# A Fourier mixing layer followed by two MLP layers: each chunk's tokens normalised and turned two chunks ahead, split one chunk ahead, one DMA each way, loads three chunks ahead

## The chip, the cores and the metric

One core of one Trainium2 chip runs the whole program. The metric is device time in microseconds (us), here that of the one core, the median of the runs shown.

The engines are TensorE (PE in the rows; its weight loads are PEld), VectorE (DVE), ScalarE (ACT), GpSimd (POOL) and SyncE (SP). Every DMA of this kernel is issued by SP. Each engine takes its instructions in the order in which the program lists them: an instruction that waits holds up everything listed behind it on that engine.

## What is computed

Two batches of 3136 tokens with 256 features pass through three layers. Cut to what matters:

```python
# 1: a filter in the frequency domain, along the tokens
X = rfft(x, axis=1)
Yr, Yi = shrink(Xr @ w_r - Xi @ w_i + b_r), shrink(Xr @ w_i + Xi @ w_r + b_i)
x = irfft(Yr + 1j * Yi, n=3136, axis=1)
# 2: normalise each token, MLP with 1024 hidden units, residual
xn = (x - mean) / sqrt(var + 1e-6) * g_ln
x = x + relu(xn @ w_ch1) @ w_ch2
# 3: 2-D Fourier transform over tokens and features, real part added, then as 2 without g_ln
u = x + real(fft(fft(x, axis=1), axis=2))
un = (u - mean) / sqrt(var + 1e-6)
return u + relu(un @ w2_ch1) @ w2_ch2
```

## The kernel before, in words

**Tiling.** The 6272 tokens are 49 tiles of 128. An MLP works on chunks of up to four tiles: `mlp1` (layer 2) has the chunks numbered 0 to 12 here, `mlp2` (layer 3) those numbered 13 to 25; most have four tiles, some three or two. Products are made in split precision: a value is held as a high part and a low part, and TensorE multiplies the parts one by one (lines 222 to 224).

**One chunk on TensorE.** `l1` makes eight groups of six matmuls with 512 columns (L222 to L224, into `psa`, three buffers). ScalarE evacuates each group with the relu (L686), VectorE then makes the low part (L687). `l2` makes, for each tile, eight pairs of matmuls (L703, L704, into `psb`), which VectorE adds to the residual (L707, L708). `store` sends the tile out (L716). On TensorE the order is: first two tiles of `l2` of chunk k, three groups of `l1` of chunk k+1, the other tiles of `l2`, five groups of `l1`. So between the last `l1` matmul of a chunk and the first of the next lie two `l2` tiles.

**What a chunk needs first.** `load` fetches its tokens `y` (L594), into a ring of four buffers; the buffer of chunk c was that of chunk c−4 and comes free when the last residual of c−4 is added. In `mlp2` each pair of tiles is read from the columns of `dX` and its mirror image as separate pieces of 64 and 128 KB, and a front end adds the transform: `Front.load` fetches `r` (L751/753), `stage_b` multiplies (L767), `dmix` multiplies again (L792) and adds into `y` on VectorE (L799 to L804; L801 is the first tile of a pair, L804 the mirrored one). Then `stats` (L604, L605), `norm` (four small VectorE steps L613 to L616, two ScalarE passes per tile L624 and L625 into `q`), `flip` (two 32x32 block transposes on VectorE, L640; each half stored to a scratch array `dT`, L644, and loaded back transposed, L646), and `trans`, the split (high part on ScalarE through L204, with a scaling pass L660 in `mlp1`; low part on VectorE, L212, both into `u0r`). Chunk 0 is transposed by TensorE instead (L668).

**Beside the chunks.** Around chunks 8 to 10 and 14 to 16 the token transform of layer 3 runs in steps (`Stage98`): loads `r<-dX`, POOL L371 to L373, a ScalarE copy L204 `u0r<-w`, matmuls L222 to L224 into `psc`, stores `dA<-o`. Around chunks 0 to 3 the inverse transform of layer 1 for batch 1 still runs (matmuls L322, stores `dY` L328 to L330), from which chunks 6 and later are loaded.

**What sets the order.** `run_mlp` emits the work of chunk k with the preparation of chunk k+1 attached by small tables (`STAGE_B_AT`, `DMIX_AT`, `STATS1_AT`, `STATS2_AT`, `LATE1`, `LATE2`), and loads chunk k+2. A scheduler then simulates a timeline and lists each engine's instructions as its model finds them ready; so an instruction may stand far ahead of where it was emitted.

Of the kernel before, what the change touches and what calls it, by code (L numbers as in the profile page):

```python
# [62 lines left out]
NF = DFF // 128  # L63
# [101 lines left out]
def fourier_moe_kernel(ctx, tc, x, w_r, w_i, b_r, b_i, g_ln, w11, w12, w21, w22,  # L165
# [415 lines left out]
    class Chunk:  # L581
# [25 lines left out]
        def norm(self):  # L607
# [13 lines left out]
            for i in range(nt):  # L621
                o, v = self.yn[:, i, :], y[:, i, :]
                if self.by_act:
# [3 lines left out]
                if not self.flipped:  # L627
                    o, v = (o.rearrange("p (h c j) -> p h j c", h=2, j=4), v.rearrange("p (h j c) -> p h j c", h=2, j=4))
# [4 lines left out]
        def flip(self, h):  # L633

            x = self.nt * 32
            if h == 0:
                self.d = next(dT_ring)
                self.xt, self.z = qslot(F32), qslot(F32)
            z = self.z[:, h * 512:h * 512 + 4 * x]
# [3 lines left out]
            dh = self.d[h][0:512 * x].rearrange("(p f) -> p f", p=128)  # L643
            sp.dma_start(out=dh, in_=z)  # L644
            v = bass.AP(dh.tensor, dh.offset, [[x, 128], [128 * x, 4], [1, x]])
            sp.dma_start(out=self.xt[:, h * 512:h * 512 + 4 * x].rearrange("p (i x) -> p i x", i=4), in_=v)  # L646

        def trans(self, c):
# [5 lines left out]
            if self.flipped:  # L654
                v = "p (i q t) -> p i q t"
                ps = self.xt[:, c * 512:c * 512 + n].rearrange("p (q i t) -> p i q t", q=4, t=32)
# [17 lines left out]
        def l1(self, f):  # L674
# [11 lines left out]
            nc.scalar.activation(out=h[:, 0:n], in_=ps[:, 0:n], func=AF.Relu)  # L686
# [211 lines left out]
    mlp1[0].flipped = False  # L898
# [34 lines left out]
    def run_mlp(chunks, nxt, hooks):  # L933

        allc = chunks + nxt
        for k, ch in enumerate(chunks):
            n = allc[k + 1] if k + 1 < len(allc) else None
            at = {}

            def put(part, i, f, *a):  # L940
                at.setdefault((part, i), []).append(lambda: f(*a))

            if n is not None and n.front is not None:
                i = 0
                for p, pr in enumerate(n.front.pairs):
                    put("l1", STAGE_B_AT[p], n.front.stage_b, p)
                    put("l1", DMIX_AT[p], n.front.dmix, p, n.y, i)
                    w = 2 if pr[0][1] else 1
                    for t in range(w):
                        put("l1", STATS2_AT[p], n.stats, i + t)  # L950
                    i += w
                late = LATE2
            elif n is not None:
                def stats(t, ch=ch, n=n):
                    with ExitStack() as es:
                        if ch is mlp1[0]:
                            es.enter_context(tc.issue_after(ch.rest[STATS1_AT[t]]))
                        n.stats(t)

                for t in range(4):  # L960
                    put("l1", STATS1_AT[t], stats, t)
                late = LATE1
            if n is not None:
                for (part, i), f, a in zip(late, (n.norm, n.flip, n.flip, n.trans, n.trans), ((), (0,), (1,), (0,), (1,))):
                    put(part, min(i, ch.nt - 1) if part == "l2" else i, f, *a)
# [65 lines left out]
    run_mlp(mlp1, mlp2[0:2], hooks)  # L1031
# [41 lines left out]
```

## Time and profile before

| | us |
|---|---|
| runs of the kernel before | 876.9, 877.44, 882.62 |
| their median | 877.44 |
| the profiled execution: its own time | 876.97 |
| the profiled execution: span of its trace | 875.2 |
| TensorE busy in the span | 812.8 |
| VectorE busy | 535.9 |
| ScalarE busy | 360.1 |
| POOL busy | 120.2 |

A span is the time from the first to the last instruction in the trace. In timeline rows the first number is the start in us, the second the duration, `x2` means that two like instructions in a row are shown as one, and the bracket at the end tells how long the engine was idle just before and what ended that. A matmul row can overlap the next, since matmuls are pipelined: their rate is read from the distance of starts.

### The profile page before, as it was taken

The page shows a single profiled execution, that of the slowest core. Times are in us where ns is not written, and L with a number is a line of the kernel's source. Part 1 is how long each engine was busy: PE and PEld are TensorE (multiplying, and loading weights), DVE is VectorE, ACT ScalarE, POOL GpSimd, SP SyncE. Part 2 cuts the span into 40 slices and gives each one's busy share as a digit, 9 for nine tenths or more (in the row PEclk, how much of TensorE's full clock was granted, in tenths as well). Part 3 has the DMA queues.
Part 4 walks back from the last instruction along what each step waited for, and adds up shares of the span by engine and source line. Part 5 has one row for each costly group of instructions (what it writes and reads, how often), then busy time and mean ns, then how long its engine had stood idle before and what let it go on. Part 6 is the DMA issues. An engine that isn't in the chain of part 4 may idle for free.

```text
span 875.2 us, 12158 instructions
## 1 busy us (share of the span) xinstructions
PE 812.8 (93%) x4268; PEld 672.4 (77%) x4268; DVE 535.9 (61%) x1262; ACT 360.1 (41%) x793; POOL 120.2 (14%) x152
## 2 busy tenths in 40 slices
PE   9999999989899999999999999988998888787996
PEld 4888878756778889887787877866886777676885
DVE  6589984597474678867576426525565655444432
ACT  1332465379374322552324325444455344132221
POOL 1112312300000000344100045353000000000000
PEclk9999999999989999999998999999999989999999
DMA  8641103414852122645422243533444321221001
GB/s 245 209 132 62 50 1 123 173 37 156 265 187 97 49 73 85 193 142 174 156 83 90 74 109 105 168 125 104 146 126 128 114 92 34 88 73 48 25 25 35
DMA packets 81777, 96.23 MB, mean 110 GB/s; under 512 B 17442, under 2 KB 60714, under 8 KB 81520
## 3 DMA queue, kind: packets, MB, share of 16 engines
q1 hardware_dynamic: 81716, 95.45, 35.1%
q8 instruction: 34, 0.56, 0.3%
q14 instruction: 27, 0.22, 0.1%
HBM read 57.41 MB, written 38.01 MB: 109 GB/s over the span
## 4 chain that ended last, share of the span: by engine, by line
PE 51%; DMA 20%; DVE 13%; ACT 6%; SPq 4%; POOL 3%; issue 2%; ACTq 0%; POOLq 0%; DVEq 0%
PE psb L703 13%; PE psa L222 7%; PE psb L704 7%; PE psa L223 6%; PE psa L224 6%; DMA yb<-dX 6%; DMA r<-dX 4%; PE psb L482 4%; DMA dT<-q 3%; DMA q<-dT 2%; DMA dA<-o 2%; DVE h L687 2%; SPq L328 2%; PE psc L303 2%; PE psa L450 2%
## 5 line engine op out<-in xcount | busy, mean ns | idle before, releaser
L686 ACT ACTIVATE h<-psa 128x512 fp32r<-128x512 f32 (+2 forms) x208 | 115.2, 570 | 205.5 <-PE psa L224 144.6
L687 DVE SCALAR_TENSOR_TENSOR h<-psa,h 128x512 fp32r<-128x512 f32 (+2 forms) x208 | 133.4, 651 | 76.8 <-ACT h L686 75.4
L703 PE MATMUL psb<-r2b,h 128*128 128x512 f32 x392 | 145.6, 416 | 7.0 <-ACT h L686 7.0
L703 PE MATMUL psb<-r3a,h 128*128 128x512 f32 x392 | 136.8, 397 | 1.4 <-ACT h L686 1.1
L222 PE MATMUL psa<-u0r,r2b 128*128 128x512 f32 (+2 forms) x208 | 84.9, 408 | 27.6 <-DVE h L687 27.1
L704 PE MATMUL psb<-r2b,h 128*128 128x256 f32 x392 | 108.8, 290 | 0.0
L704 PE MATMUL psb<-r3a,h 128*128 128x256 f32 x392 | 106.0, 283 | 0.8 <-DVE h L687 0.8
L703 PEld LDWEIGHTS psb<-r2b,h 128*128 128x128 f32 x392 | 76.3, 199 | 24.5 <-ACT h L686 8.3
L482 PE MATMUL psb<-wm,h 128*128 128x256 f32 (+1 forms) x600 | 88.8, 298 | 0.8 <-DVE w L488 0.8
L703 PEld LDWEIGHTS psb<-r3a,h 128*128 128x128 f32 x392 | 71.8, 188 | 17.5 <-ACT h L686 1.4
L222 PE MATMUL psa<-u0r,r3a 128*128 128x512 f32 (+2 forms) x192 | 77.4, 403 | 7.2 <-DVE h L687 7.0
L482 PEld LDWEIGHTS psb<-wm,h 128*128 128x128 f32 (+1 forms) x600 | 76.1, 189 | 8.6 <-issue 8.0
L223 PE MATMUL psa<-u0r,r2b 128*128 128x512 f32 (+2 forms) x208 | 82.1, 394 | 0.0
L704 PEld LDWEIGHTS psb<-r2b,h 128*128 128x128 f32 x392 | 78.2, 200 | 3.8
L224 PE MATMUL psa<-u0r,r2b 128*128 128x512 f32 (+2 forms) x208 | 81.1, 392 | 0.0
L704 PEld LDWEIGHTS psb<-r3a,h 128*128 128x128 f32 x392 | 73.6, 189 | 6.1 <-DVE h L687 1.5
L223 PE MATMUL psa<-u0r,r3a 128*128 128x512 f32 (+2 forms) x192 | 74.3, 387 | 0.0
L224 PE MATMUL psa<-u0r,r3a 128*128 128x512 f32 (+2 forms) x192 | 74.0, 387 | 0.0
L707 DVE TENSOR_TENSOR o<-psb,yb 128x256 f32<-128x256 f32 x74 | 29.5, 415 | 67.4 <-PE psb L704 67.3
L222 PEld LDWEIGHTS psa<-u0r,r2b 128*128 128x128 f32 x208 | 41.1, 197 | 37.0 <-DVE h L687 29.1
L204 ACT ACTIVATE yg<-psc 98x512 f32<-98x512 f32 (+2 forms) x58 | 48.3, 856 | 40.2 <-PE psc L502 26.7
L222 PEld LDWEIGHTS psa<-u0r,r3a 128*128 128x128 f32 x192 | 37.4, 195 | 17.6 <-DVE h L687 10.9
(125 smaller groups left out, 1292.3 us busy)
## 6 DMA issues: line engine op xcount, KB each, us to landing
dT<-q SPq DMA_DIRECT2D x42, 256.0 KB
q<-dT SPq DMA_DIRECT2D x42, 256.0 KB
s<-in_moe_w_ch_dram SPq DMA_DIRECT2D x16, 512.0 KB
r<-dX SPq DMA_DIRECT2D x32, 196.0 KB
dA<-o SPq DMA_DIRECT2D x32, 196.0 KB
dY<-yg SPq DMA_DIRECT2D x12, 512.0 KB
r<-dA SPq DMA_DIRECT2D x48, 128.0 KB
dX<-o SPq DMA_DIRECT2D x11, 512.0 KB
```

The costliest lines, as they stand in the source:

```text
L204: nc.scalar.activation(out=o, in_=i, func=AF.Copy, scale=scale)
L222: nc.tensor.matmul(out=ps, lhsT=lh, rhs=rh, start=first, stop=False)
L223: nc.tensor.matmul(out=ps, lhsT=ll, rhs=rh, start=False, stop=False)
L224: ins = nc.tensor.matmul(out=ps, lhsT=lh, rhs=rl, start=False, stop=last)
L303: nc.tensor.matmul(out=ps, lhsT=cam, rhs=self.raw[g // 2][:, e * 512:(e + 1) * 512], start=True, stop=True)
L328: sp.dma_start(out=dY[self.b][16 * c:16 * c + 16, :], in_=v[c:96:6, :])
L482: nc.tensor.matmul(out=ps[0:m, u * D:(u + 1) * D], lhsT=xv[:, o:o + m], rhs=wm_hl[wv][:, e, c, :], start=k == 0, stop=k == 11)
L686: nc.scalar.activation(out=h[:, 0:n], in_=ps[:, 0:n], func=AF.Relu)
L687: ins = nc.vector.scalar_tensor_tensor(out=l[:, 0:n], in0=ps[:, 0:n], scalar=0.0, in1=h[:, 0:n], op0=ALU.max, op1=ALU.subtract)
L703: nc.tensor.matmul(out=ps, lhsT=h[:, ts_], rhs=w2[:, f, :], start=f == 0, stop=False)
L704: nc.tensor.matmul(out=ps[:, 0:D], lhsT=l[:, ts_], rhs=w2[:, f, 0:D], start=False, stop=f == NF - 1)
L707: nc.vector.tensor_tensor(out=o, in0=ps[:, 0:D], in1=self.y[:, i, :], op=ALU.add)
```

## The change

The preparation of a chunk is taken apart. Statistics, front end, `norm` and `flip` are emitted two chunks ahead, with new table entries; the split is emitted one chunk ahead, behind the last evacuation (L687 of group 7) of the chunk before it; the load is emitted three chunks ahead, at the end of a chunk. `flip` stores and loads both halves with one DMA each way (512 KB where there were two of 256 KB). Chunk 1 is transposed by TensorE like chunk 0: eight more 128x128 matmuls and no `flip`. Line numbers of the changed kernel are 1 to 5 higher at the places below (L640 stays, L687 is L692, L707 is L712, L801 and L804 are L806 and L809, L212 is L213).

```diff
-STAGE_B_AT = (0, 1)
-DMIX_AT = (2, 3)
+STAGE_B_AT = (1, 3)
+DMIX_AT = (3, 5)
 STATS1_AT = (0, 1, 2, 3)
-STATS2_AT = (3, 4)
-LATE1 = (("l1", 4), ("l1", 5), ("l1", 6), ("l2", 0), ("l2", 1))
-LATE2 = (("l1", 5), ("l1", 6), ("l1", 7), ("l2", 1), ("l2", 2))
+STATS2_AT = (4, 6)
+NORM_AT = (4, 7)
+FLIP_AT = (1, 2)
+TRANS_AT = (0, 0)
...
         def flip(self, h):
...
-            dh = self.d[h][0:512 * x].rearrange("(p f) -> p f", p=128)
-            sp.dma_start(out=dh, in_=z)
-            v = bass.AP(dh.tensor, dh.offset, [[x, 128], [128 * x, 4], [1, x]])
-            sp.dma_start(out=self.xt[:, h * 512:h * 512 + 4 * x].rearrange("p (i x) -> p i x", i=4), in_=v)
+            if h == 0:
+                return
+            d = next(dT_ring).rearrange("h f -> (h f)")[0:1024 * x]
+            sp.dma_start(out=d.rearrange("(h p f) -> p h f", h=2, p=128),
+                         in_=self.z[:, 0:8 * x].rearrange("p (h f) -> p h f", h=2))
+            self.xt = qslot(F32)
+            sp.dma_start(out=self.xt[:, 0:8 * x].rearrange("p (i x) -> p i x", i=8),
+                         in_=bass.AP(d.tensor, d.offset, [[x, 128], [128 * x, 8], [1, x]]))
...
-    mlp1[0].flipped = False
+    mlp1[0].flipped = mlp1[1].flipped = False
...
-            n = allc[k + 1] if k + 1 < len(allc) else None
+            n, m, far = (allc[k + d] if k + d < len(allc) else None for d in (1, 2, 3))
...
+            def split(c, ch=ch, n=n):
+                with tc.issue_after(ch.relu), tc.issue_after(ch.rest[NF - 1]):
+                    n.trans(c)
+
+            if n is not None and n.flipped:
+                for c in range(2):
+                    put("l2", TRANS_AT[c], split, c)
+            todo = [m]
+            if n is mlp1[1]:
+                todo = [n, m]
+            for n_ in todo:
...
+                put("l1", NORM_AT[two], n_.norm)
+                if n_.flipped:
+                    for h in range(2):
+                        put("l2", FLIP_AT[h], n_.flip, h)
+                else:
+                    for c in range(2):
+                        put("l2", ch.nt - 1, n_.trans, c)
...
-            if k + 2 < len(allc):
-                allc[k + 2].load()
             for i in range(ch.nt):
                 ch.l2(i)
                 ch.store(i)
...
+            if far is not None:
+                far.load()
...
-    run_mlp(mlp1, mlp2[0:2], hooks)
+    mlp1[2].load()
+    run_mlp(mlp1, mlp2[0:3], hooks)
```

**Place 1, VectorE, the front end of chunk 25.** Before, these rows stand in `l2` of chunk 21, whose tiles are the L707/L708 rows; L801, L804 and L604 belong to chunk 25, whose `y` takes over the buffer that those L707 read.

```order
L707 TENSOR_TENSOR o<-psb,yb 128x256 x2
L708 TENSOR_TENSOR o<-psb,o 128x256 x2
L801 TENSOR_TENSOR yb<-w,yb 128x256
L604 BN_STATS st<-yb 128x6
L605 BN_AGGR mv<-st 128x2
L707 TENSOR_TENSOR o<-psb,yb 128x256
L804 TENSOR_TENSOR yb<-w,yb 128x256
L708 TENSOR_TENSOR o<-psb,o 128x256
L604 BN_STATS st<-yb 128x6
L687 SCALAR_TENSOR_TENSOR h<-psa,h 128x512 x2
```

In the changed kernel the rows of chunk 25 stand in `l2` of chunk 22 (the L712/L713 rows) and behind the first evacuation of chunk 23 (the L692 at the top).

```order
L692 SCALAR_TENSOR_TENSOR h<-psa,h 128x512
L208 COPY w<-psc 128x2
L208 COPY w<-w 128x1
L804 TENSOR_TENSOR w<-w,psc 128x127
L805 TENSOR_TENSOR w<-w,psc 128x127
L806 TENSOR_TENSOR yb<-w,yb 128x256
L809 TENSOR_TENSOR yb<-w,yb 128x256
L605 BN_STATS st<-yb 128x6 x2
L712 TENSOR_TENSOR o<-psb,yb 128x256
```

The addition into the mirrored tile (L804, now L809) moved from the chunk whose buffer its `y` inherits to the chunk after that; the chunks before it, 20 to 24, read alike.

**Place 2, VectorE, the split of chunk 25.** Before, the split (L212) stands ahead of the last evacuation of chunk 23: these are that chunk's evacuations, and its first `l2` tiles behind them.

```order
L687 SCALAR_TENSOR_TENSOR h<-psa,h 128x512 x4
L212 TENSOR_TENSOR u0r<-q,u0r 128x256 x2
L687 SCALAR_TENSOR_TENSOR h<-psa,h 128x512
L707 TENSOR_TENSOR o<-psb,yb 128x256 x2
L708 TENSOR_TENSOR o<-psb,o 128x256 x2
```

In the changed kernel it stands behind the last evacuation of chunk 24.

```order
L692 SCALAR_TENSOR_TENSOR h<-psa,h 128x512 x5
L213 TENSOR_TENSOR u0r<-q,u0r 128x256 x2
L712 TENSOR_TENSOR o<-psb,yb 128x256 x2
L713 TENSOR_TENSOR o<-psb,o 128x256 x2
L692 SCALAR_TENSOR_TENSOR h<-psa,h 128x256
```

The split moved later by one chunk and one evacuation, to the last place ahead of the chunk that reads it (the 256-wide L692 is that chunk's first evacuation).

**Place 3, VectorE, the first statistics of batch 1's later chunks.** Before, the statistics of chunk 6 (the L604 rows, `yb` loaded from `dY`) stand in `l2` of chunk 1.

```order
L687 SCALAR_TENSOR_TENSOR h<-psa,h 128x512
L640 STREAM_TRANSPOSE q<-q 128x4x4x32 x2
L687 SCALAR_TENSOR_TENSOR h<-psa,h 128x512
L707 TENSOR_TENSOR o<-psb,stg 128x256 x2
L708 TENSOR_TENSOR o<-psb,o 128x256 x2
L604 BN_STATS st<-yb 128x6 x3
L605 BN_AGGR mv<-st 128x2 x2
L604 BN_STATS st<-yb 128x6 x2
```

In the changed kernel they stand at the beginning of `l2` of chunk 2.

```order
L692 SCALAR_TENSOR_TENSOR h<-psa,h 128x512 x5
L640 STREAM_TRANSPOSE q<-q 128x4x4x32 x2
L213 TENSOR_TENSOR u0r<-w,u0r 128x512 x2
L605 BN_STATS st<-yb 128x6 x3
L712 TENSOR_TENSOR o<-psb,u0r 128x256
L606 BN_AGGR mv<-st 128x2 x2
L712 TENSOR_TENSOR o<-psb,u0r 128x256
```

They moved by seven evacuations of chunk 2, about one run of `l1`; the stores of `dY` that the loads wait for moved too, since batch 1's last inverse steps now end ahead of the second tile of chunk 1's `l2` instead of during its `l1`.

On SP the loads of a `mlp2` chunk's `y` stay where they were, among the stores of chunk c−4; between them stand the one store to `dT` and, two or three rows later, the one load from it. Each engine has about as many instructions as before, ScalarE somewhat fewer.

## Rows read from the trace of the kernel before

**Rows 1.** The page: the span and the first engine's busy time, share, instructions.

```profile
span 875.2 us, 12158 instructions
...
PE 812.8 (93%) x4268; PEld 672.4 (77%) x4268; DVE 535.9 (61%) x1262; ACT 360.1 (41%) x793; POOL 120.2 (14%) x152
```

**Rows 2.** By stretch: length; busy of PE, PEld, DVE, ACT, POOL; granted clock; DMA.

```profile
256.00:356.00 100.00, 99.72 (x541) 86.90 (x540) 68.45 (x146) 34.64 (x72) 0.00 (x0) 1.00 0.25 81
...
715.00:806.00 91.00, 75.22 (x357) 62.38 (x356) 42.90 (x112) 28.55 (x66) 0.00 (x0) 0.92 0.23 70
```

**Rows 3.** What TensorE waited for: line, awaited; total us, times, longest us.

```profile
PE psa L222 <- DVE h L687: 34.3, 12, 5.0
```

**Rows 4.** Timeline of TensorE: five of the nine long waits.

```profile
242.44 0.79 PE L222 MATMUL psa<-u0r,r3a 128*128 128x512 f32 x1 [4.07 <-DVE h L687]
...
477.19 0.79 PE L222 MATMUL psa<-u0r,r3a 128*128 128x512 f32 x1 [2.07 <-DVE h L687]
...
671.20 0.79 PE L222 MATMUL psa<-u0r,r2b 128*128 128x512 f32 x1 [4.31 <-DVE h L687]
...
697.61 0.44 PE L222 MATMUL psa<-u0r,r2b 128*128 128x384 f32 x1 [3.46 <-DVE h L687]
...
793.80 0.73 PE L222 MATMUL psa<-u0r,r2b 128*128 128x512 f32 x1 [4.98 <-DVE h L687]
```

**Rows 5.** Timeline of VectorE around the last of them.

```profile
786.03 0.42 DVE L707 TENSOR_TENSOR o<-psb,yb 128x256 f32<-128x256 f32 x1 [1.24 <-PE psb L704]
792.06 0.42 DVE L804 TENSOR_TENSOR yb<-w,yb 128x256 f32<-128x256 f32 x1 [5.61 <-DMA yb<-dX]
```

**Rows 6.** Timeline of SP: the load that this L804 waited for.

```profile
783.88 0.55 SPq L594 DMA_DIRECT2D yb<-dX  x1
```

**Rows 7.** VectorE's idle time ahead of line 804: total us, times.

```profile
  DMA yb<-dX: 26.2, 6
```

**Rows 8.** Timeline of TensorE: two `l2` tiles, then matmuls behind the wait.

```profile
783.02 0.39 PE L703 MATMUL psb<-r2b,h 128*128 128x512 f32 x1
...
788.55 0.28 PE L704 MATMUL psb<-r2b,h 128*128 128x256 f32 x1
...
797.31 0.40 PE L224 MATMUL psa<-u0r,r2b 128*128 128x512 f32 x1
797.55 0.39 PE L222 MATMUL psa<-u0r,r2b 128*128 128x512 f32 x1
```

**Rows 9.** Timeline of VectorE at the first long wait.

```profile
238.54 1.08 DVE L604 BATCH_NORM_STATS2 st<-yb 128x6 f32<-128x256 f32 x3 [6.21 <-DMA yb<-dY]
```

**Rows 10.** Timeline of SP: a store to `dT` and its load, other loads between.

```profile
660.75 1.06 SPq L644 DMA_DIRECT2D dT<-q  x2
661.85 0.45 SPq L751 DMA_DIRECT2D r<-dA  x1
666.86 0.37 SPq L646 DMA_DIRECT2D q<-dT  x1
```

**Rows 11.** Timeline of ScalarE: three waits behind which relus stood.

```profile
473.87 0.63 ACT L204 ACTIVATE u0r<-q 128x512 fp32r<-128x512 f32 x1 [6.89 <-DMA q<-dT]
...
574.60 0.63 ACT L204 ACTIVATE u0r<-w 98x512 fp32r<-98x512 f32 x1 [7.33 <-POOL w L373]
...
669.42 0.52 ACT L204 ACTIVATE u0r<-q 128x384 fp32r<-128x384 f32 x1 [7.81 <-DMA q<-dT]
```

**Rows 12.** Timeline of TensorE: the two long waits on the relu.

```profile
575.77 0.80 PE L703 MATMUL psb<-r2b,h 128*128 128x512 f32 x1 [3.36 <-ACT h L686]
...
610.49 0.80 PE L703 MATMUL psb<-r2b,h 128*128 128x512 f32 x1 [3.62 <-ACT h L686]
```

**Rows 13.** Timeline of VectorE: the low part of a split.

```profile
475.84 0.69 DVE L212 TENSOR_TENSOR u0r<-q,u0r 128x512 fp32r<-128x512 f32 x1 [0.29 <-ACT u0r L204]
```

**Rows 14.** The page's groups: busy time, mean ns of one, idle before, releaser.

```profile
L686 ACT ACTIVATE h<-psa 128x512 fp32r<-128x512 f32 (+2 forms) x208 | 115.2, 570 | 205.5 <-PE psa L224 144.6
L687 DVE SCALAR_TENSOR_TENSOR h<-psa,h 128x512 fp32r<-128x512 f32 (+2 forms) x208 | 133.4, 651 | 76.8 <-ACT h L686 75.4
```

More of the change, by code (lines that the diff above doesn't have):

```diff
@@ L622, in norm @@
                 o, v = self.yn[:, i, :], y[:, i, :]
+                if not self.flipped:
+                    o, v = (o.rearrange("p (h c j) -> p h j c", h=2, j=4), v.rearrange("p (h j c) -> p h j c", h=2, j=4))
                 if self.by_act:
@@ L626, in norm @@
                     continue
-                if not self.flipped:
-                    o, v = (o.rearrange("p (h c j) -> p h j c", h=2, j=4), v.rearrange("p (h j c) -> p h j c", h=2, j=4))
                 eng = nc.gpsimd if i in APPLY_POOL and self is mlp1[0] else nc.vector
@@ L636, in flip @@
             if h == 0:
-                self.d = next(dT_ring)
-                self.xt, self.z = qslot(F32), qslot(F32)
-            z = self.z[:, h * 512:h * 512 + 4 * x]
+                self.z = qslot(F32)
+            z = self.z[:, h * 4 * x:(h + 1) * 4 * x]
             nc.vector.transpose(out=z.rearrange("p (j i t) -> p i j t", j=4, t=32),
@@ L655, in trans @@
                 v = "p (i q t) -> p i q t"
-                ps = self.xt[:, c * 512:c * 512 + n].rearrange("p (q i t) -> p i q t", q=4, t=32)
+                ps = self.xt[:, c * n:(c + 1) * n].rearrange("p (q i t) -> p i q t", q=4, t=32)
                 h, l = (a[:, c, 0:n].rearrange(v, q=4, t=32) for a in (self.xh, self.xl))
@@ L685, in l1 @@
             h, l = hl[:, 0:512], hl[:, 512:1024]
-            nc.scalar.activation(out=h[:, 0:n], in_=ps[:, 0:n], func=AF.Relu)
+            ins = nc.scalar.activation(out=h[:, 0:n], in_=ps[:, 0:n], func=AF.Relu)
+            self.relu = getattr(ins, "ins", ins)
             ins = nc.vector.scalar_tensor_tensor(out=l[:, 0:n], in0=ps[:, 0:n], scalar=0.0, in1=h[:, 0:n],
@@ L936, in run_mlp @@
         for k, ch in enumerate(chunks):
-            n = allc[k + 1] if k + 1 < len(allc) else None
+            n, m, far = (allc[k + d] if k + d < len(allc) else None for d in (1, 2, 3))
             at = {}
             def put(part, i, f, *a):
[L941 to L962, printed above, removed]
@@ L963, in run_mlp @@
-            if n is not None:
-                for (part, i), f, a in zip(late, (n.norm, n.flip, n.flip, n.trans, n.trans), ((), (0,), (1,), (0,), (1,))):
-                    put(part, min(i, ch.nt - 1) if part == "l2" else i, f, *a)
+                at.setdefault((part, min(i, ch.nt - 1) if part == "l2" else i), []).append(lambda: f(*a))
+            def split(c, ch=ch, n=n):
[4 more added lines that the diff above has]
+                    put("l2", TRANS_AT[c], split, c)
@@ new lines, in run_mlp, with stats @@
+            todo = [m]
+            if n is mlp1[1]:
+                todo = [n, m]
+            for n_ in todo:
+                if n_ is None:
+                    continue
+                two = n_.front is not None
+                if two:
+                    i = 0
+                    for p, pr in enumerate(n_.front.pairs):
+                        put("l1", STAGE_B_AT[p], n_.front.stage_b, p)
+                        put("l1", DMIX_AT[p], n_.front.dmix, p, n_.y, i)
+                        w = 2 if pr[0][1] else 1
+                        for t in range(w):
+                            put("l1", STATS2_AT[p], n_.stats, i + t)
+                        i += w
+                else:
+                    def stats(t, ch=ch, n_=n_):
+                        with ExitStack() as es:
+                            if ch is mlp1[0]:
+                                es.enter_context(tc.issue_after(ch.rest[STATS1_AT[t]]))
+                            n_.stats(t)
+                    for t in range(4):
+                        put("l1", STATS1_AT[t], stats, t)
+                put("l1", NORM_AT[two], n_.norm)
+                if n_.flipped:
+                    for h in range(2):
+                        put("l2", FLIP_AT[h], n_.flip, h)
+                else:
+                    for c in range(2):
+                        put("l2", ch.nt - 1, n_.trans, c)
```

## The prediction

> **What bounds the kernel now.** I read the page first. TensorE is busy for 812.8 of 875.2 us, 93%, and no other engine comes near [rows 1]. So TensorE is the bound, and what a change can win is the time in which it stands still or runs slowly. The table by stretches tells where that is. From 256 to 356 us TensorE is busy for 99.72 of 100 us at full clock: an undisturbed stretch of chunks wastes nothing. From 715 to 806 us it is busy for 75.22 of 91, at a mean clock of 0.92 [rows 2].
>
> Next the list of what TensorE waited for. One row holds most: the first matmul of an `l1` group waiting for VectorE's evacuation L687, 34.3 us in 12 waits [rows 3]. Nine are long, 33.2 us together (the other three make 1.1); five are shown, and the four left out lie in the late stretch between the last two shown [rows 4]. An evacuation is short work, so the question is what stood ahead of it on its engine. The timelines around the waits answer:
>
> - The six from 697.61 to 793.80. In the last one SP issues a load of `y` at 783.88 [rows 6]. VectorE ends a residual addition at 786.45, then is idle for 5.61 us until that load has landed, and only at 792.06 makes L804, the addition into the mirrored tile of chunk 25 [rows 5]. L708 and two L687 are queued behind it (place 1 of the order). Issue to use is 792.06 − 783.88 = 8.2 us. The view of that line confirms that it is one mechanism: six waits, 26.2 us of idle VectorE [rows 7].
> - 242.44: the same with `bn_stats`, which is listed ahead of the evacuations and waits 6.21 us for a load from `dY` [rows 9].
> - 477.19 and 671.20: ScalarE's first step of a split waits 6.89 and 7.81 us for the flipped tokens to come back [rows 11]; relus are queued behind it, so L687 is late as well. At 671.20 the store to `dT` was issued at 660.75 and SP could send the load only at 666.86 [rows 10].
>
> Each long wait has a second cost. Behind that of 793.80 the granted clock is at the lower level: nine matmuls start from 793.80 to 797.31, eight distances in 3.51 us, 0.44 each, against 0.24 from 797.31 to 797.55 [rows 4, 8]. That is 8 × 0.2 = 1.6 us. The mean clock of 0.92 over 91 us says that 2 × 0.08 × 91 = 14.6 us were spent at the lower level in a stretch with four long waits and the slow matmuls behind them, so 3.6 us for each [rows 2]. Matmuls that run at half speed lose half of that, 1.8. I take 1.8 us for each wait; the example's 1.6 is the lower bound, and 2 the upper, were all nine like the worst.
>
> **The change, part by part.**
>
> *Front end and statistics two chunks ahead, loads three ahead.* The buffer ring still has four places, so loads cannot come much earlier; SP keeps them among the stores of chunk c−4. What moves is the consumer: L804 of chunk 25 stood one residual addition behind the one that frees its buffer, and now stands a whole chunk later (place 1 of the order). The first and the last matmul of two `l2` tiles start at 783.02 and 788.55; with 0.1 for the last, two tiles take 5.6 us [rows 8]; a chunk of four tiles is twice that plus 48 `l1` matmuls at 0.24, 11.2 + 11.5 = 22.7 us. A load that needs 8.2 us has 22 to do it. Six waits go: 26.2 us of VectorE's idle time, 22.8 of TensorE's (the six are 33.2 less 4.07, 2.07, 4.31) [rows 4, 7].
>
> *Split behind the last evacuation.* A split that waits can no longer hold up evacuations of the chunk before. The flip of a chunk is emitted in `l2` two chunks ahead; up to the split lie about two `l2` tiles and one run of `l1`, 5.6 + 11 = 16.6 us. The slow case took from 660.75 to 669.42, 8.7 us [rows 10, 11]. So the waits of 477.19 and 671.20 go too, 6.4 us.
>
> Its new price: nothing but two `l2` tiles, 5.6 us, now lies between the last `l1` matmul and the first that needs the split. Behind that matmul come a relu (0.57), the last L687 (0.65), two ScalarE copies (0.63 each) and two L212 (0.69 each) [rows 11, 13, 14]. ScalarE needs 0.57 + 2 × 0.63 = 1.8, VectorE ends at 0.57 + 0.65 + 2 × 0.69 = 2.6, or 3.2 if a copy is late. In `mlp1` two scaling passes make it about 4. Slack: 2.4 us, and 1.5 in `mlp1`. I cost it at nothing. If the cover were gone, each chunk would stand still for the whole chain.
>
> *One DMA each way.* Fewer issues on SP (twenty-odd chunks × 2). Off the path while the flip has its 16 us: zero; bounds from one issue saved (1.06 for two, so 0.5 us [rows 10]) to the load coming later by half of the 6.1 us from the stores to the load's issue, 3 us of a slack of 8 [rows 10].
>
> *Chunk 1 on TensorE, chunk 2 beside it.* Eight small matmuls. By the nearest rows they lie between 0.24 of a 512-column matmul and 0.79 of a slow one [rows 4, 8]: 2 to 6 us if none overlaps; I take 2, since they replace nothing. The statistics of chunk 6 move back by one run of `l1`, about 11 us, but so do the inverse's last steps and with them the `dY` stores and the loads (place 3 of the order). The lead stays what it was, between a wait gone (0) and the 6.21 us of now [rows 9]; I put back 3, so that of 4.07 + 1.8 about 3 remains gained.
>
> *The token transform around chunks 14 to 16.* Its two waits, 3.36 and 3.62, come from ScalarE's copy waiting for POOL (7.33 at 574.60) [rows 11, 12]. The change moves other work around them, not their loads. I leave them; bounds: they and their slow matmuls go (7.0 + 3.6 = 10.6 us), or they grow by as much.
>
> **The sum.** Nine waits 33.2 and 9 × 1.8 = 16.2: −49.4. Added: +2 (transposes), +3 (chunk 6), +1 (places where more work stands ahead of an evacuation near chunk 8). Span 875.2 − 43.4 = 831.8. The profiled execution took 876.97, 1.8 more than its span, and is within 0.5 us of the median 877.44; so **833.6 us**. Its own range, with the terms' bounds: 820 to 850.
>
> One rule would put the gain elsewhere. The load of 783.88 brings 128 KB and is not used before 8.2 us later [rows 5, 6]. The Trainium skill ("DMA: Bandwidth & Descriptors", Anatomy of one DMA) fits 2.0 us plus bytes over 436 GB/s for a DMA, an estimate of 2.3 us here, measured on the other descriptor path. By it the load would be there before L804's turn, there would be no wait to remove and the sum would lose 22.8 + 10.8; the trace differs, and decides.
>
> **Rivals.**
>
> *The token transform's waits go as well, and the start costs nothing.* For it: the split no longer shares ScalarE's queue with the steps ahead of the last evacuation. Against: POOL and its loads stay. 833.6 − 10.6 − 5 = 818. Chance 0.15.
>
> *SP gives back a third to half.* A load from `dT` waits on SP for its store: 666.86 against 661.85 + 0.45, 4.6 us [rows 10]. In the changed order the next `y` loads stand behind it. With a lead of 22 us less 8.2 there is room for two such waits, so only loads that also meet the transform's would be late. Half of the 33.6 us for the six waits comes back: about 850; or the statistics of chunks 6 to 9 stall in a row, 6.21 each for two more, the same size. Chance 0.15. The same page of the Trainium skill says that a DMA's semaphore wait is done by the issuing sequencer ahead of dispatch; SP's 4.6 us agree.
>
> *The split becomes a stall in each chunk.* This is the other side. If from the last `l1` matmul to the end of the split it takes more than 5.6 us, TensorE stops once per chunk, 24 times. What could stretch it: front-end steps that stand ahead of the split on VectorE and wait for a `dmix` product, or flipped tokens that are not back. At 1.8 us late per chunk the 43 us are used up; at 2.2, or 7.8 us of chain, 24 × 2.2 = 53 and the kernel is slower by over 1%, 886. Against: 2.6 to 4 us by rows. Chance 0.07.
>
> *The load is what is late, wherever its consumer stands.* If loads are issued later in the new order than the buffer allows, behind stores that wait for residuals, the wait only moves: within 1%, about 874. The order of SP speaks against it. Chance 0.06.
>
> **How the numbers follow.** My forecast has 0.57, lying within 820 to 850. Faster by over 1% (below 868.7; about 1% is what can be told from no change here): 0.57 + 0.15 + 0.15 = 0.87. Same 0.06, slower 0.07. For 8 in 10 I take the forecast's own range and go down to 814 for the first rival and up to 857 for the second; outside are the last two, 0.13, and some of the edges.
>
> **What would show it.** In the profile after: no wait of L809 for `yb<-dX` above 1 us; TensorE's wait on VectorE's evacuation below 10 us instead of 34.3; the stretch before the last chunks as dense as 256 to 356, clock 1.00. A wait of ScalarE on POOL near chunks 14 to 16 still there. For the split: the first `l1` matmul of a chunk follows the second `l2` tile without a wait on ScalarE's or VectorE's `u0r`. If TensorE's waits list `u0r` with two dozen entries, the third rival is right; if L809 still waits, the fourth.

## The result, and the profile after

The changed kernel takes 819.25 us (median of four runs, 817.12 to 819.83) against 877.17 us of the kernel before, timed beside it: a ratio of 0.933, 95% interval 0.928 to 0.938. The forecast was 833.6 with a range of 814 to 857 and 0.87 for faster by over 1%. Direction and mechanism held; the gain is 58 us where 43 were forecast.

The page of the kernel after: span, busy time of the engines, and TensorE's granted clock in 40 slices (9 is 0.9 or more).

```profile
span 817.4 us, 12025 instructions
...
PE 791.3 (97%) x4276; PEld 658.9 (81%) x4276; DVE 538.9 (66%) x1260; ACT 364.1 (45%) x791; POOL 120.2 (15%) x152
...
PEclk9999999999999999999999999999989999999999
```

The work is nearly the same; TensorE's busy time fell by 21.5 us all the same [rows 1]. The granted clock accounts for that (see the last section): one slice in 40 is left below 0.9. By stretch, in the columns of [rows 2]:

```profile
530.00:590.00 60.00, 60.00 (x322) 50.85 (x320) 34.78 (x87) 31.94 (x69) 28.69 (x49) 1.00 0.48 141
590.00:625.00 35.00, 28.92 (x126) 23.18 (x124) 15.23 (x34) 12.66 (x28) 3.75 (x8) 0.85 0.41 118
...
720.00:810.00 90.00, 90.00 (x496) 77.92 (x495) 47.90 (x122) 31.09 (x72) 0.00 (x0) 1.00 0.21 56
```

The last 90 us answer to the stretch of 75.22 busy us in 91 [rows 2]: now 90.00 of 90 at clock 1.00. The stretch 530 to 590, the token transform of batch 1 among the chunks, is full as well. Nearly all that TensorE still loses in layer 3, by standing still or at the lower clock, lies between 590 and 625. What TensorE waited for, the longest two entries (line, awaited; total us, times, longest):

```profile
PE psc L772 <- DMA r<-dA: 4.8, 2, 4.3
PE psa L223 <- DVE h L692: 4.0, 4, 1.9
```

34.3 us of waits on VectorE's evacuation [rows 3] became 4.0, and a wait on a load of the front end is new. The view of L809 (L804 before) has no releaser under "sat idle", where 26.2 us in six waits stood [rows 7]:

```profile
L809 DVE TENSOR_TENSOR yb<-w,yb x24: 412/419/420, 445.4 to 755.1; 128x256 f32<-128x256 f32 x24
its engine sat idle before it (us, times) until:
who waited for it (us, times):
```

Now the end of a late chunk, which shows the split in its new place. ScalarE, VectorE and TensorE between chunks 23 and 24:

```profile
765.76 0.60 ACT L690 ACTIVATE h<-psa 128x512 fp32r<-128x512 f32 x1 [0.76 <-PE psa L225]
766.25 1.14 ACT L205 ACTIVATE u0r<-q 128x512 fp32r<-128x512 f32 x2
```

```profile
766.39 0.69 DVE L692 SCALAR_TENSOR_TENSOR h<-psa,h 128x512 fp32r<-128x512 f32 x1 [0.67 <-ACT h L690]
767.00 1.28 DVE L213 TENSOR_TENSOR u0r<-q,u0r 128x512 fp32r<-128x512 f32 x2
```

```profile
765.33 0.39 PE L225 MATMUL psa<-u0r,r2b 128*128 128x512 f32 x1
...
771.17 0.39 PE L223 MATMUL psa<-u0r,r2b 128*128 128x512 f32 x1
```

The last `l1` matmul of chunk 23 starts at 765.33; the split is done at 768.28; the first `l1` matmul of chunk 24 starts at 771.17. A chain of 2.9 us stands in a cover of 5.8, and 2.9 are to spare.

Where the gain lies in the program, by the start of the last `l2` matmul of a chunk in either trace (us):

| after chunk | before | changed | gain so far | gain in the part |
|---|---|---|---|---|
| 2 | 265.8 | 261.7 | 4.1 | 4.1 |
| 14 | 555.9 | 542.8 | 13.1 | 9.0 |
| 16 | 624.4 | 603.7 | 20.7 | 7.6 |
| 17 | 654.4 | 637.2 | 17.2 | −3.5 |
| 25 | 867.8 | 810.3 | 57.5 | 40.3 |

The parts do not cut the work quite alike. By the traces, 12, 15 and 12 `l1` matmuls of the next chunk stand ahead of the last `l2` tile of chunks 14, 16 and 17 in the changed kernel, and none in the kernel before; at 0.23 us each that is 2.8 to 3.5 us made one part earlier.

### The profile page after: what moved, and what is told of

The parts are those of the page before. It is cut to its first block, busy times and chain, and to the rows that moved or that the text cites. A ratio compares the mean times of both kernels' runs of the same rounds, so it can differ in the third digit from the quotient of the medians.

```text
span 817.4 us, 12025 instructions
## 1 busy us (share of the span) xinstructions
PE 791.3 (97%) x4276; PEld 658.9 (81%) x4276; DVE 538.9 (66%) x1260; ACT 364.1 (45%) x791; POOL 120.2 (15%) x152
## 4 chain that ended last, share of the span: by engine, by line
PE 76%; DMA 9%; DVE 8%; ACT 3%; SPq 2%; issue 1%; POOL 1%; ACTq 0%; POOLq 0%
PE psb L708 20%; PE psb L709 10%; PE psa L223 10%; PE psa L224 10%; PE psa L225 9%; PE psb L483 4%; PE psc L772 3%; PE psc L323 2%; PE psc L304 2%; PE psc L503 2%; PE psc L797 1%; DMA cb<-in_cb_dram 1%; PE psa L451 1%; DMA h<-in_x_dram 1%; DMA r<-dA 1%
## 5 line engine op out<-in xcount | busy, mean ns | idle before, releaser
L692 DVE SCALAR_TENSOR_TENSOR h<-psa,h 128x512 fp32r<-128x512 f32 (+2 forms) x208 | 134.4, 654 | 91.5 <-ACT h L690 89.9
L708 PE MATMUL psb<-r3a,h 128*128 128x512 f32 x392 | 137.5, 399 | 0.6 <-DVE o L713 0.6
L708 PE MATMUL psb<-r2b,h 128*128 128x512 f32 x392 | 137.7, 398 | 0.0
L709 PE MATMUL psb<-r2b,h 128*128 128x256 f32 x392 | 106.0, 281 | 0.0
L708 PEld LDWEIGHTS psb<-r3a,h 128*128 128x128 f32 x392 | 71.6, 188 | 16.8 <-issue 1.5
L708 PEld LDWEIGHTS psb<-r2b,h 128*128 128x128 f32 x392 | 71.9, 188 | 14.7
L223 PE MATMUL psa<-u0r,r2b 128*128 128x512 f32 (+2 forms) x208 | 81.9, 394 | 0.0
L224 PE MATMUL psa<-u0r,r2b 128*128 128x512 f32 (+2 forms) x208 | 80.0, 385 | 0.0
L225 PE MATMUL psa<-u0r,r2b 128*128 128x512 f32 (+2 forms) x208 | 79.6, 384 | 0.0
L709 PEld LDWEIGHTS psb<-r2b,h 128*128 128x128 f32 x392 | 73.9, 189 | 3.2
L712 DVE TENSOR_TENSOR o<-psb,yb 128x256 f32<-128x256 f32 x74 | 30.6, 422 | 69.2 <-PE psb L709 68.4
L223 PE MATMUL psa<-u0r,r3a 128*128 128x512 f32 (+2 forms) x176 | 67.1, 382 | 4.0 <-DVE h L692 4.0
L224 PE MATMUL psa<-u0r,r3a 128*128 128x512 f32 (+2 forms) x176 | 66.2, 376 | 0.0
L225 PE MATMUL psa<-u0r,r3a 128*128 128x512 f32 (+2 forms) x176 | 63.8, 380 | 0.0
L213 POOL TENSOR_TENSOR h<-w 128x512 f32<-128x512 f32 (+1 forms) x26 | 34.1, 1314 | 109.9 <-DVE w L490 76.4
```

The source lines that it names most:

```text
L213: ins = eng.tensor_tensor(out=o, in0=a, in1=b, op=ALU.subtract)
L223: nc.tensor.matmul(out=ps, lhsT=lh, rhs=rh, start=first, stop=False)
L224: nc.tensor.matmul(out=ps, lhsT=ll, rhs=rh, start=False, stop=False)
L225: ins = nc.tensor.matmul(out=ps, lhsT=lh, rhs=rl, start=False, stop=last)
L692: ins = nc.vector.scalar_tensor_tensor(out=l[:, 0:n], in0=ps[:, 0:n], scalar=0.0, in1=h[:, 0:n], op0=ALU.max, op1=ALU.subtract)
L708: nc.tensor.matmul(out=ps, lhsT=h[:, ts_], rhs=w2[:, f, :], start=f == 0, stop=False)
```

## The experiments

Each run was timed in turns with the kernel before on one chip; the chips differ by half a per cent or so, so ratios to the kernel before are compared, and a difference of 0.01 is some 9 us.

**The changed kernel once more.** No edit.

> The changed kernel once more, unaltered, timed against the kernel before on the chip of this call, since the variants were timed on other chips than it. If the time of a chip only scales both kernels, the ratio is 0.933 again, within 0.929 to 0.937; then e1 (0.9329) is the same as the changed kernel, e4 (0.9379) 4 us slower and e8 (0.9251) 7 us faster. If it comes out at 0.926 or below, e8 and e12 have gained nothing.

Measured: 818.68 us, ratio 0.936 (0.933 to 0.939), within what was expected. The two measurements of the changed kernel, 0.933 and 0.936, are what the others are read against.

**Three buffers for `y`.** The lead of the loads shrinks by a chunk. The scheduler made its lists anew: from 520 us on VectorE's order differs in a few places, by a neighbour or two; ahead of that more steps moved.

```diff
-        yield from ring(cp.tile([128, YB * 1024], F32, tag="cw", name="yb"), YB, 1024)
+        yield from ring(cp.tile([128, YB * 1024], F32, tag="cw", name="yb"), 3, 1024)
```

> The changed kernel with three buffers for y in place of four; nothing is moved on VectorE, so a chunk's load has one chunk less of lead. Theory 1 (the gain of the late stretch is the distance between the release of a buffer and L809): L806/L809 stand right behind the release again, wait 3 to 6 us once or twice per chunk of layer 3, TensorE's waits on VectorE's evacuation are back at 30 us or more, and the time rises from 819 by 30 to 70 us. Theory 2 (the gain came from the rearranged flip, split and fewer DMAs): rises by less than 6 us.

Measured: 849.25 us, ratio 0.964 (0.958 to 0.970). VectorE's and TensorE's waits:

```profile
DVE yb L809 <- DMA yb<-dX: 43.7, 11, 6.7
```

```profile
PE psa L223 <- DVE h L692: 21.7, 10, 3.8
```

The waits are back at once, eleven of them, with flip, split and DMAs as changed; seven of the eleven, the four longest among them, lie behind 680 us, where VectorE's order is nearly the same. By the ratios 25 to 28 us are lost, about half of the gain and less than the 30 to 70 expected. TensorE's waits stayed under the expected 30 us as well; that three `psa` buffers and the `l2` tiles cover a part of VectorE's waits is likely, and not shown.

**The kernel before with the front end pinned.** One rule, in the emission of `dmix`:

```diff
-                    put("l1", DMIX_AT[p], n.front.dmix, p, n.y, i)
+                    def dmix(p, y, i, f=n.front, old=allc[k - 1] if k else None):
+                        with ExitStack() as es:
+                            if old is not None:
+                                es.enter_context(tc.issue_after(old.rest[0]))
+                            f.dmix(p, y, i)
+
+                    put("l1", DMIX_AT[p], dmix, p, n.y, i)
```

> The kernel before with one addition: the dmix steps of a layer-3 chunk may not stand on VectorE ahead of the first evacuation of the chunk two before it (they stood up to three chunks before). Flip, split, loads, two DMAs each way and chunk 1 stay as they were. Theory 1 (distance to the release): the six late waits go and with them 33 us (22.8 of waits, 10.8 of slow matmuls); the waits at 242, 477, 576, 610 and 671 stay: 838 to 850. Theory 2 (flip, split and DMAs made the gain): within 10 us of 877.

Measured: 854.31 us, ratio 0.969 (0.963 to 0.975). TensorE's wait on the evacuation:

```profile
PE psa L222 <- DVE h L687: 12.7, 7, 4.6
```

L804 has no wait left. So a later place on VectorE is enough to remove the six late waits: nothing was emitted or loaded earlier, or merged (the rule holds back VectorE's steps of `dmix`; the scheduler listed the other engines anew around them). The gain, 26 us, falls 4 us short of the bottom of what was expected. In the same trace VectorE's splits wait longer:

```profile
DVE u0r L212 <- ACT u0r L204: 63.3, 22, 7.4
```

In the trace of the kernel before the same entry is smaller:

```profile
DVE u0r L212 <- ACT u0r L204: 39.2, 18, 6.6
```

**The same, and the split held behind the last evacuation.** Two rules of order on the kernel before, nothing else.

```diff
+                def split(c, ch=ch, n=n):
+                    with tc.issue_after(ch.relu), tc.issue_after(ch.rest[NF - 1]):
+                        n.trans(c)
+
+                if n.flipped:
+                    late = late[0:3] + (("l2", 0), ("l2", 0))
-                for (part, i), f, a in zip(late, (n.norm, n.flip, n.flip, n.trans, n.trans), ((), (0,), (1,), (0,), (1,))):
+                for (part, i), f, a in zip(late, (n.norm, n.flip, n.flip, split, split), ((), (0,), (1,), (0,), (1,))):
```

> The kernel before with two rules of order and nothing else: the dmix steps not ahead of the first evacuation of the chunk two before, and the split not ahead of the last evacuation of the chunk before. Emission one chunk ahead, old tables, two DMAs each way, chunk 1 flipped. Theory 1 (what a VectorE or ScalarE list has right behind a DMA is all that matters): the waits at 477 and 671 go as well as the six late ones; those at 242, 576 and 610 stay: 835 to 845, ratio 0.95 to 0.96. Theory 2 (the emission two chunks ahead is needed for the flips to be back in time): no better than with the first rule alone, ratio 0.97.

Measured: 835.0 us, ratio 0.949 (0.945 to 0.953). The two rules make 45 of some 57 us. What stays is the wait on relus behind the token transform, and a little at the start:

```profile
PE psb L704 <- ACT h L686: 8.3, 3, 4.7
PE psa L222 <- DVE h L688: 8.0, 7, 2.8
```

**The changed kernel without the hold on the split.**

```diff
-                with tc.issue_after(ch.relu), tc.issue_after(ch.rest[NF - 1]):
-                    n.trans(c)
+                n.trans(c)
```

> The changed kernel without the rule that the split stands behind the last evacuation; the scheduler then lists the splits of late chunks on VectorE six or so evacuations earlier, in the l2 of the chunk two before. Theory 1 (an early split waits for the flipped tokens, with relus and evacuations behind it on the same engines): ScalarE waits for q<-dT several times, 2 to 5 us each, and the time rises by 10 to 30 us. Theory 2 (the place of the split is indifferent once flips are two ahead): 816 to 822.

Measured: 854.21 us, ratio 0.968 (0.963 to 0.973): 30 us are lost. ScalarE's waits on flipped tokens, TensorE's two longest entries, and its only wait on a relu:

```profile
ACT u0r L205 <- DMA q<-dT: 63.0, 13, 7.9
```

```profile
PE psa L223 <- DVE h L692: 12.0, 8, 4.7
PE psc L797 <- ACT w L205: 10.2, 4, 5.3
PE psb L708 <- ACT h L690: 1.1, 1, 1.1
```

The scheduler lists a split where its model has the flipped tokens back; in the trace they come later, 13 times, and front-end copies, relus and evacuations queue behind. Without the hold, two chunks of lead keep only about half of the gain: for the split, the early list place eats the lead.

**Layer 3 prepared one chunk ahead.** For chunks with a front end the old tables, the split not held; layer 2 and the loads three chunks ahead as changed.

```diff
+            if n is not None and n.front is not None:
...
+                    put("l1", (0, 1)[p], n.front.stage_b, p)
+                    put("l1", (2, 3)[p], n.front.dmix, p, n.y, i)
...
+                put("l1", 5, n.norm)
+                put("l1", 6, n.flip, 0)
+                put("l1", 7, n.flip, 1)
+                put("l2", 1, n.trans, 0)
+                put("l2", 2, n.trans, 1)
-            if n is not None and n.flipped:
+            elif n is not None and n.flipped:
...
-            todo = [m]
+            todo = [m if m is not None and m.front is None else None]
```

> The changed kernel, but the chunks of layer 3 are prepared one chunk ahead with the old tables and without holding the split back. Theory 1: the scheduler lists L806/L809 right behind the release again, their waits for yb<-dX are back, 20 us or more, and so are the two waits on ScalarE behind the token transform (3 to 4 us each): 850 to 868. Theory 2: under 830.

Measured: 864.21 us, ratio 0.981 (0.977 to 0.986). VectorE's waits for `y` are back though the loads are still emitted three chunks ahead. TensorE waits on a relu behind the token transform again, once, 2.2 us (before: 3.36 and 3.62 us [rows 12]); the other wait of the entry below stands behind flipped tokens:

```profile
DVE yb L809 <- DMA yb<-dX: 17.5, 5, 5.7
DVE yb L806 <- DMA yb<-dX: 15.6, 5, 6.8
```

```profile
PE psb L708 <- ACT h L690: 4.8, 2, 2.7
```

**Layer 2 prepared one chunk ahead**, from chunk 2 on, its split not held; layer 3 as changed.

```diff
+            if n is not None and n.front is None and n.flipped:
...
+                put("l1", 4, n.norm)
+                put("l1", 5, n.flip, 0)
+                put("l1", 6, n.flip, 1)
+                put("l2", 0, n.trans, 0)
+                put("l2", 1, n.trans, 1)
...
-            todo = [m]
+            todo = [m if m is not None and m.front is not None else None]
```

> The changed kernel, but chunks of layer 2 from chunk 2 on are prepared one ahead with the old tables and the split not held; layer 3 as changed. Theory 1: layer 2 had two long waits before (242 and 477 us, 6.1 us and as much of slow matmuls); the second belongs to layer 3's chunk 13 and stays gone, the first comes back in full: 4 to 8 us more than 819. Theory 2 (layer 2's rearrangement carries a good part of the gain): 832 or more.

Measured: 828.05 us, ratio 0.938 (0.933 to 0.943), so 2 to 4 us more than the changed kernel, at the edge of what can be told, and not the full 4 to 8 us that theory 1 asked. The wait of the start is back in full, as expected, 4.5 us:

```profile
PE psa L223 <- DVE h L692: 8.0, 5, 4.5
```

Layer 2's part of the change carries little.

**Two DMAs each way per flip again.**

```diff
-            if h == 0:
-                return
...
+            dh = self.d[h][0:512 * x].rearrange("(p f) -> p f", p=128)
+            sp.dma_start(out=dh, in_=z)
+            v = bass.AP(dh.tensor, dh.offset, [[x, 128], [128 * x, 4], [1, x]])
+            sp.dma_start(out=self.xt[:, h * 4 * x:(h + 1) * 4 * x].rearrange("p (i x) -> p i x", i=4), in_=v)
```

> The changed kernel with two DMAs each way per flip again (each half stored and loaded by itself), all else as changed. Theory 1: the flip has some 16 us and needs less than 10, so the number of DMAs decides nothing: 817 to 823. Theory 2 (fewer issues on SP are what brought the loads of y and r in time): 830 or more, with L809 or the front end's matmuls waiting for loads again.

Measured: 823.12 us, ratio 0.933 (0.927 to 0.939): no difference. The number of DMAs decides nothing here.

**Chunk 19's front end later.** Its two `stage_b` steps are held behind the seventh group of chunk 17's `l1` on TensorE; in the second run behind the eighth (`ch.last` in place of `ch.six`, and the second pair, `dmix` and statistics in `l2`).

```diff
+                        late = n_.front.pairs[-1][0][1] == 0
+                        if late:
+                            def b19(p, f=n_.front, ch=ch):
+                                with tc.issue_after(ch.six):
+                                    f.stage_b(p)
+
+                            put("l1", 6 + p, b19, p)
+                            put("l1", 7, n_.front.dmix, p, n_.y, i)
...
```

> The changed kernel, but the front end of chunk 19 stands behind the seventh group of chunk 17 on TensorE in place of the fourth. In the profile after, the first of its matmuls waits 4.33 us for r<-dA at 610. Theory 1 (that load is just late, and a later consumer finds it landed): the wait goes with its slow matmuls, 6 to 8 us less than 819: 811 to 814. Theory 2 (the wait moves to the flip or split of chunk 19): 817 to 821, with a wait of 2 us or more ahead of the first l1 group of chunk 19.

> The changed kernel with chunk 19's front end behind the whole l1 of chunk 17 on TensorE (e8 had it one group earlier and kept a wait of 2.32 us). Theory 1: that wait goes too with its slow matmuls: 3 to 4 us less than e8, ratio 0.92. Theory 2 (the flip of chunk 19 is now late): a wait of 1 us or more ahead of chunk 19's l1, and no less than e8.

Measured: 813.77 us, ratio 0.925 (0.921 to 0.929), and 815.02 us, ratio 0.926 (0.922 to 0.931). Both beat the changed kernel by 6 to 9 us by the ratios; their intervals lie below that of its second measurement (from 0.933) and overlap that of its first (from 0.928). The wait in the changed kernel, on SP and on TensorE:

```profile
598.15 1.49 SPq L428 DMA_DIRECT2D dA<-o  x1
600.00 2.75 SPq L595 DMA_DIRECT2D yb<-dX  x2
603.65 0.38 SPq L649 DMA_DIRECT2D q<-dT  x1
604.25 1.05 SPq L756 DMA_DIRECT2D r<-dA  x2
```

```profile
610.41 1.08 PE L772 MATMUL psc<-cb,r 128*128 128x64 f32 x4 [4.33 <-DMA r<-dA]
```

Chunk 19 is the first that reads batch 1's transform, and needs the last rows that it stores (598.15). Their load is issued at 604.25, behind the `y` loads and one of flipped tokens. Its first reader has its turn at 606.08, where the matmul ahead of it ends, and starts 6.2 us behind the issue. In the first run the same reader comes later and waits 2.32 us, and in the second chunk 19 doesn't wait:

```profile
613.27 1.46 PE L774 MATMUL psc<-cb,r 128*128 128x64 f32 x8 [2.32 <-DMA r<-dA]
```

The second run gave no further gain, against its first theory; nor is a wait at chunk 19's `l1` in its trace, as its second would have it. Where its 3 us went stays open; the granted clock of its profiled execution is 0.987, against 0.992 in the first run.

**The split late on purpose**, to price the stall that the prediction feared. First the low parts behind the residual of the second `l2` tile, nothing held on ScalarE. In both runs a second rule ties VectorE's `dmix` steps behind a chunk's first evacuation:

```diff
-                with tc.issue_after(ch.relu), tc.issue_after(ch.rest[NF - 1]):
+                with tc.issue_after(ch.res):
                     n.trans(c)
-TRANS_AT = (0, 0)
+TRANS_AT = (1, 1)
...
+                        def dmix(p, y, i, f=n_.front, ch=ch):
+                            with tc.issue_after(ch.rest[0]):
+                                f.dmix(p, y, i)
...
```

> The changed kernel with VectorE's low parts of the split listed behind the residual additions of the second l2 tile in place of the last evacuation (front ends held at the place that they have now). Theory 1 (5.6 us of cover, 3 of them in use): the low parts end 2 us after TensorE could start the next l1, once per chunk: 24 times 2 us, with slow matmuls behind some, 40 to 90 us more than 819, and TensorE waits for u0r two dozen times. Theory 2 (the next tiles of l2 or other matmuls fill in): less than 10 us more.

Measured: 882.44 us, ratio 1.002 (0.999 to 1.005). The size is as the first theory had it, the cause isn't: `u0r` is not among TensorE's longer waits. The rule on the split holds only instructions on VectorE, so the scheduler listed ScalarE's copies early, and they waited:

```profile
ACT u0r L205 <- DMA q<-dT: 106.5, 13, 14.5
```

So this run repeats the one without the hold, and worse. The second try keeps the copies behind the last relu (`tc.issue_after(ch.relu), tc.issue_after(ch.res)`):

> As e7_split_late, but ScalarE's copies are held behind the last relu as in the changed kernel, so that VectorE's low parts alone are late, behind the residual of the second l2 tile. Theory 1: they end 2 us after TensorE could begin the next chunk, 23 times, with slow matmuls behind some: 40 to 90 us more than the changed kernel, ratio 0.98 to 1.03, and TensorE's waits on VectorE for u0r are in the list, 1.5 to 3 us each. Theory 2: hidden, ratio under 0.945.

Measured: 841.62 us, ratio 0.957 (0.953 to 0.961): 20 us more, half of the least that theory 1 asked, and more than theory 2 allowed. TensorE waits elsewhere:

```profile
PE psc L773 <- DMA r<-dA: 10.4, 2, 6.6
PE psb L708 <- DVE o L713: 9.6, 8, 5.3
```

These are its two longest entries: a load of the front end (3.8 of the 10.4 us are at chunk 19, which waits in the changed kernel too), and `psb` buffers that VectorE's residual additions free late. `u0r` is not in the list's first seven. TensorE's order had changed as well: the scheduler knew of the late split and put the third and fourth `l2` tile ahead of the next `l1`, all but one group of it. So the cover is not fixed at two tiles, and neither theory describes what happened; how much of the 20 us is the low parts' place, and how much the new lists, was not separated. What a split that is late without the scheduler's knowledge would cost was not measured.

## Why the prediction was right, and where it was off

**The six late waits: right, and shown.** The step was that L804 waits because it stands right behind the release of the buffer whose load it needs, and that moving it by a chunk removes the wait. Shortening the lead by a buffer brings the waits back (ratio 0.964); holding the `dmix` steps with L804 back in the kernel before removes them (0.969). The prediction set this against the Trainium skill ("DMA: Bandwidth & Descriptors", Anatomy of one DMA), by whose fit, made on the other descriptor path, an estimate of 2.3 us for 128 KB, nothing would have had to wait. The trace disagrees wherever the lead is short: from issue to use it was 8.2 us at 783.88 in the kernel before, and with three buffers the longest wait for such a load is 6.7 us.

**The split held back: right in kind, too small in size.** The prediction gave it the waits of 477 and 671, 6.4 us and their slow matmuls. On its own, taken out of the changed kernel, the hold is worth 30 us; added to the pinned kernel before, it is worth 17 to 18 (0.969 to 0.949). The step missed that two chunks of preparation would let the scheduler list splits early again, with more waits for flipped tokens (13, 63.0 us) than the kernel before had long ones. Its price was costed at nothing, with a chain of 2.6 to 4 us and 1.5 to 2.4 of slack; the chain of the late chunk above is 2.9 and the slack 2.9. Right: in the profile after no `l1` matmul waits for `u0r`.

**One DMA each way at zero: right** (0.933 with two).

**The token transform's waits: wrong.** I left its two waits, 7.0 us, where they were, and gave their going only 0.15 as a rival. They went: chunks 15 and 16 gained 7.6 us. Of ScalarE's two long waits for POOL there, 7.33 [rows 11] and 7.60 us, one is left, and no relu is queued close behind it; in the profile after ScalarE has

```profile
583.52 0.60 ACT L690 ACTIVATE h<-psa 128x512 fp32r<-128x512 f32 x1 [0.25 <-PE psa L225]
584.02 1.14 ACT L205 ACTIVATE u0r<-q 128x512 fp32r<-128x512 f32 x2
590.63 0.63 ACT L205 ACTIVATE u0r<-w 98x512 fp32r<-98x512 f32 x1 [5.47 <-POOL w L374]
```

The relu and the split come first, and the 5.47 us fall into the time of the `l2` tiles; TensorE loses 1.73 us there. Before, a relu stood right behind the copy of 574.60 [rows 11]:

```profile
575.13 0.58 ACT L686 ACTIVATE h<-psa 128x512 fp32r<-128x512 f32 x1
```

The waits stay in the kernel before with both rules of order, one comes back with layer 3 one chunk ahead, and without the hold TensorE has none on a relu at the transform (its one of 1.1 us is at 667, behind flipped tokens). So it is the emission two chunks ahead that moves the transform's copies off the relus, not the hold. I had looked for a change in the waited-for load, and not in what is queued behind the waiter.

**The start: terms too large.** Transposes and chunk 6 were put at +5 against 5.9 gained; up to chunk 2 the change gained 4.1. The transposes wait 2.37 us once, and of 4.07 at 242.44 [rows 4] 1.88 are left, without slow matmuls behind them. No run tells the transposes and chunk 6 apart.

**Chunks 3 to 14:** 9.0 where 2.9 were forecast (the wait of 477 less 1 for chunk 8). The wait of 477 went. Most of the rest are small waits, six between 403 and 547 of 6.5 us together, three of them of the first batch's transform, that I had listed nowhere; three of 2.5 us stand in this part now. Some 3 us more were won than the table shows, since 12 matmuls of chunk 15 are made ahead of its line.

**The late part:** 39.7 were forecast for chunks 17 to 25, 36.8 came (57.5 − 20.7). In it stands a wait that no step named, the load `r<-dA` of chunk 19, whose reader now stands too close behind its issue. Moving it away is worth 6 to 9 us. The part before, eight microseconds behind the last of its seven waits, and the part after, in the columns of [rows 2]:

```profile
624.40:867.80 243.40, 216.33 (x1137) 186.35 (x1136) 123.99 (x351) 84.56 (x207) 0.00 (x0) 0.95 0.25 76
793.80:801.80 8.00, 8.00 (x29) 6.53 (x30) 5.92 (x16) 5.28 (x12) 0.00 (x0) 0.79 0.22 66
```

```profile
603.70:810.30 206.60, 202.27 (x1107) 175.56 (x1105) 119.52 (x320) 81.08 (x190) 0.00 (x0) 0.98 0.30 85
```

TensorE stood still for 27.1 us before and for 4.3 after. Behind each of the seven waits eight microseconds have a mean clock of 0.79 to 0.81, so at most 8 × 0.21 = 1.7 us are lost: the 1.8 that I took was right. After, 10 us behind the wait of chunk 19 have a clock of 0.68, 3.2 us. So 22.8 of waits and 11.9 − 3.2 = 8.7 of slow matmuls went, 31.5 us; the other 5 are no gain of this part but work that is made ahead of its line now (30 matmuls fewer in it, 15 of them chunk 17's `l1`).

The sum by parts (to chunk 2, 14, 16 and 25): 0.9, 2.9, 0 and 39.7 forecast, 4.1, 9.0, 7.6 and 36.8 measured. By kind: TensorE's idle time fell by 36.3 us (62.4 to 26.1), its busy time by 21.5; forecast were 33.2 and 16.2, with 6 put back. So the 14 us by which the gain exceeds the forecast are the 6 that did not have to be paid, 3 of idle time and 5 of slow matmuls. The time, 819, lies just below the forecast's own range (820 to 850) and beside the 818 of the first rival, which had the transform's waits go and the start cost nothing. Both came in part, but not for the reason that it gave, the split's new place: the hold alone left those waits. The rival that ended on the other side, a stall in each chunk, did not come about: the chain was as short as its rows said. The rival by which SP gives back a part did not either; L809 never waits.

## What to carry to other kernels

An engine takes its list in order, so what a wait costs is decided by what stands behind the waiter: put work that needs a fresh transfer a full stage behind its issue and behind, not ahead of, the evacuations that the bounding engine needs. Where a scheduler makes the list by a model, more lead in the emission is not enough, since it lists the consumer as early as its model allows; two rules of order on the kernel before gave 45 of some 57 us. And whoever moves a consumer earlier should look for the producer that then is last: here one load in 26 chunks cost 6 to 9 us.

## What the runs showed of the hardware

The lower clock does not follow every wait alike. Behind the wait of 1.88 us at 242.87 in the changed kernel the matmuls soon start 0.23 us apart, as before it:

```profile
242.87 0.50 PE L223 MATMUL psa<-u0r,r3a 128*128 128x512 f32 x1 [1.88 <-DVE h L692]
243.21 0.39 PE L224 MATMUL psa<-u0r,r3a 128*128 128x512 f32 x1
243.44 0.40 PE L225 MATMUL psa<-u0r,r3a 128*128 128x512 f32 x1
```

The same wait of the same chunk, 1.83 us in the first run with chunk 19's front end later, is followed by slow ones, 0.42 apart:

```profile
245.07 0.61 PE L223 MATMUL psa<-u0r,r3a 128*128 128x512 f32 x1 [1.83 <-DVE h L694]
245.48 0.63 PE L224 MATMUL psa<-u0r,r3a 128*128 128x512 f32 x1
245.90 0.63 PE L225 MATMUL psa<-u0r,r3a 128*128 128x512 f32 x1
```

Behind the 1.73 us at 591.99 in the changed kernel they are slow too, and so they are behind 4.33 us at 610.41, where two successive ones start 0.43 apart:

```profile
593.78 0.63 PE L224 MATMUL psa<-u0r,r2b 128*128 128x512 f32 x1
594.21 0.63 PE L225 MATMUL psa<-u0r,r2b 128*128 128x512 f32 x1
...
613.10 0.63 PE L225 MATMUL psa<-u0r,r2b 128*128 128x512 f32 x1
613.53 0.63 PE L223 MATMUL psa<-u0r,r2b 128*128 128x512 f32 x1
```

So whether a wait of this length brings slow matmuls is not settled by its length, and a forecast that counts on either is a guess.

In all, the mean granted clock rose from 0.967 to 0.992, and TensorE's busy time fell by 21.5 us for nearly the same matmuls (4268 before, 4276 now). The clock gives the same size: 0.033 × 875.2 less 0.008 × 817.4 is 22.3 us. A good third of the gain of 58 us lies in that, beside the waits themselves.
